# A new order for the first microseconds, and a shorter head weighting, in a linear-attention and Mish kernel

## The chip, the cores and the metric

The kernel runs on one core of a Trainium2 chip. The metric is the device time of one execution in microseconds (us); lower is better. A core has TensorE (PE in the profile; PEld is its weight load), VectorE (DVE), ScalarE (ACT), GpSimd (POOL) and SyncE (SP, which here only issues DMAs). Each engine works through its own list of instructions in order, and waits where an instruction needs a result that another engine or a DMA hasn't delivered.

## The reference

The input `x` has 2048 rows of 512 numbers. The kernel computes `x + A(xn) + B(xn)` in bf16.

```
xn = layernorm(x)                                   # (x - mean) / sqrt(var + 1e-5)
# A: linear attention, 32 heads of 16
q, k, v = split(xn @ wqkv)
pq, pk  = q @ w_phi[h],  k @ w_phi[h]               # a 16x16 matrix per head
phi     = concat(softmax(p), softmax(-p))           # 32 features, for q and for k
kv, z   = sum_s phi_k^T v,  sum_s phi_k
A       = concat_heads(phi_q kv / (phi_q z + 1e-6)) @ wo
# B: a dense layer with Mish, width 1792
B       = mish(xn @ w1 + b1) @ w2
```

## The kernel before, in words

The 2048 rows are 16 tiles of 128 rows, in four groups of four. The order of all work is written out by hand: each engine's list follows the order of the calls in the source, and a PSUM bank comes from a pool (`bank`, L66) in a fixed rotation `turns`, so that TensorE waits when the bank whose turn it is hasn't been read out.

The projection of q and k is folded with the per-head matrices: `fold` (L105) multiplies the transposed weight `wT` by a block-diagonal matrix `Wbd` (made at L477 from `block`, a mask, and `wsrc`, the loaded `w_phi`) and copies four PSUM banks into `wkp`. From then on `project(wkp, t)` (L163) gives the logits of tile t directly, and `logits` (L203) copies them to `p_sb`.

**The head** (L443 to L511) deals with group 0. After the DMAs are issued, GpSimd makes the identity and the mask, and TensorE runs twelve matmuls on the identity that nobody reads (L471). `ln_stats` (L122) takes mean and variance on VectorE for two tiles at a time, and GpSimd turns the variance into 1/sqrt by an addition and a power (L131, L134). `ln_apply` (L137) normalises on VectorE. Then come the fold of the k weights (three casts on ScalarE, one on VectorE), `ln_turn_pe` (L149: four transposes of a tile on TensorE into one bank, then a copy to `xnT`), and the logits of the four tiles. Next VectorE takes the statistics of group 1, starts `extremes(0)` (L211: the maximum and the minimum of each run of 16 logits, then the differences `e`) and in the middle of it normalises group 1, which a DMA transposes (L158). In the meantime TensorE computes the values of four tiles and five units of the hidden layer (`hidden`, L183: four matmuls, then a Mish on ScalarE, L196, which reads the bank). There are 56 such units in all. TensorE can be at most as many units ahead of ScalarE as there are banks.

**First half** (L513 to L557): for each group, ScalarE takes the exponentials of `e` (L244), VectorE divides by the sums (`normalise`, L258), TensorE accumulates k and v (L290), and projections, hidden units and the statistics of later groups fill the rest.

**Second half** (L560 to L652): `attend(h, i)` (L324) multiplies the transposed query features by the accumulated matrix into a four-bank tile `pnd`. ScalarE copies out of it first the 32 features' numerators `nm` (L347, which lands in the buffers of `wkp` or `wv`), then the denominators `ds` (L348). `combine(h)` (L350) works on VectorE, in two parts of one tile or in one part of two: products `u` of the denominators (L370), their sum `w` (L373), its reciprocal (L376), weights `u` again (L379, an instruction per tile), the same weights written twice side by side as `f` in bf16 (L382), `nm` times `f` (L389), and the sum of the two planes (L396). A DMA then transposes the result into `ob` (L399). `second_layer` (L407, L415) and `project_out` (L420, L424) accumulate into one bank per tile, and `residual` (L430, L432) adds it to x on VectorE. All sixteen output tiles leave by DMA (L440).

Of the kernel before, what the change touches and what calls it, by code (L numbers as in the profile page):

```python
# [13 lines left out]
ALU = mybir.AluOpType  # L14
# [4 lines left out]
def kernel(  # L19
# [68 lines left out]
    wo_sb = wqk[:, :, D : 2 * D]  # L88
    ident = consts.tile([P, P], BF16, name="ident")
    mhalf = consts.tile([P, TPG], FP32, name="mhalf")  # L90
    block = consts.tile([P, 8, 16], BF16, name="block")
    KVmask = consts.tile([P, 34], FP32, name="KVmask")
    vext = [vpool.tile([P, TPG, 4, 4, 36], BF16, name=f"vext{i}") for i in range(2)]
# [8 lines left out]
        nc.sync.dma_start_transpose(out=wT[:], in_=A_wqkv[:, base_col : base_col + D])  # L102
        return wT

    def fold(wT, dst, dve):  # L105

        for kt in range(KT):
            pf = bank("pfold")
            for j in range(4):
                nc.tensor.matmul(  # L110
                    pf[:, j * P : (j + 1) * P],
                    lhsT=wT[:, j, kt * P : (kt + 1) * P],
                    rhs=Wbd[:, j, :],
                    start=True,
                    stop=True,
                )
            if kt in dve:
                nc.vector.tensor_copy(dst[:, kt, :], pf[:])
            else:
                nc.scalar.copy(dst[:, kt, :], pf[:])  # L120

    def ln_stats(t0, n):  # L122

        stats = lnp.tile([P, TPG, nc.vector.BN_STATS_DIM], FP32, name="stats")
        mv = lnp.tile([P, TPG, nc.vector.BN_AGGR_DIM], FP32, name="mv")
        rstd = lnp.tile([P, TPG], FP32, name="rstd")
        for i in range(n):
            nc.vector.bn_stats(stats[:, i, :], x_sb[:, t0 + i, :])  # L128
        for i in range(n):
            nc.vector.bn_aggr(mv[:, i, :], stats[:, i, :])  # L130
        nc.gpsimd.tensor_scalar(  # L131
            out=rstd[:, 0:n], in0=mv[:, 0:n, 1], scalar1=1e-5, scalar2=None, op0=ALU.add
        )
        nc.gpsimd.tensor_tensor(out=rstd[:, 0:n], in0=rstd[:, 0:n], in1=mhalf[:, 0:n], op=ALU.pow)  # L134
        return mv, rstd
# [24 lines left out]
            in_=xn[:, i : i + 2, :].rearrange("p t c -> p (t c)"),  # L160
        )

    def project(w, t, pp=None):  # L163

        if pp is None:
            pp = bank("pproj")[:]
        for kt in range(KT):
            nc.tensor.matmul(  # L168
                pp, lhsT=xnT[:, t, kt, :], rhs=w[:, kt, :],
                start=(kt == 0), stop=(kt == KT - 1),  # L170
            )
        return pp
# [151 lines left out]
    def attend(h, i):  # L324

        if i == 0:
            nd_of[h] = (
                (wkp, wv)[h % 2][:].rearrange("p (i l) c -> p i l c", i=2),
                opool.tile([P, 2, 2, 4, 4, 4], FP32, name="ds"),
            )  # L330
        nm, ds = nd_of[h]
        pnd = later[0].tile([P, 4, 512], FP32, name="pnd", tag="nd")
        for pl in range(2):
            for j in range(4):
                for r in range(4):
# [11 lines left out]
        nc.scalar.copy(to, a[:, :, :, :, 0:32])  # L347
        nc.scalar.copy(ds[:, i], a[:, :, :, :, 32:36])  # L348

    def combine(h, parts=(slice(0, 2),)):  # L350

        nm, ds = nd_of.pop(h) if parts[-1].stop == 2 else nd_of[h]
        ds = ds[:].rearrange("p i l j r (x h) -> p i l x (j r) h", x=2)
        if h not in oT_of:
            ob = lnp.tile([P, 4, 512], BF16, name="ob", tag="xn")
            u = opool.tile([P, 2, 2, 32], FP32, name="u")
            w = opool.tile([P, 2, 32], FP32, name="w")
            f = opool.tile([P, 2, 2, 32, 2], BF16, name="f")
            tmp_of[h] = ob[:, 0:2, :], u, w, f
            oT_of[h] = ob[:, 2:4, :].rearrange("p i (j c) -> p (i j) c", c=P)  # L360
        o_t, u, w, f = tmp_of[h]
        for q in parts:
            n = q.stop - q.start
            uh = u[:, q].rearrange("p i l (c h) -> p i l c h", h=2)
            wh = w[:, q, None, :].to_broadcast([P, n, 2, 32]).rearrange(
                "p i l (c h) -> p i l c h", h=2
            )
            for i in range(n):
                k = q.start + i
                nc.vector.tensor_tensor(  # L370
                    out=uh[:, i], in0=ds[:, k, :, 0], in1=ds[:, k, ::-1, 1], op=ALU.mult
                )
            nc.vector.tensor_tensor(  # L373
                out=w[:, q], in0=u[:, q, 0, :], in1=u[:, q, 1, :], op=ALU.add
            )
            nc.vector.reciprocal(w[:, q], w[:, q])  # L376
            for i in range(n):
                k = q.start + i
                nc.vector.tensor_tensor(  # L379
                    out=uh[:, i], in0=ds[:, k, ::-1, 1], in1=wh[:, i], op=ALU.mult  # L380
                )
            nc.vector.tensor_copy(  # L382
                f[:, q].rearrange("p i l c o -> p (i l c) o"),
                u[:, q].rearrange("p i l (c o) -> p (i l c) o", o=1).to_broadcast(
                    [P, n * 64, 2]
                ),
            )
# [8 lines left out]
            nc.vector.tensor_tensor(  # L396
                out=o_t[:, q], in0=nm[:, q, 0, :], in1=nm[:, q, 1, :], op=ALU.add
            )
# [54 lines left out]


    make_identity(nc, ident[:])

    nc.gpsimd.memset(block[:], 1.0)
    for sign in (1, -1):
# [5 lines left out]
    nc.gpsimd.memset(mhalf[:], -0.5)  # L464
    for i in range(2):
        nc.gpsimd.memset(vext[i][:, :, :, :, 32:36], 1.0)
    dve, act = nc.vector.tensor_copy, nc.scalar.copy

    warm = bank("warm")
    for _ in range(12):  # L470
        nc.tensor.matmul(  # L471
            warm[:].rearrange("p (k c) -> p k c", k=4), lhsT=ident[:], rhs=ident[:, None, :].to_broadcast([P, 4, P]),
            start=True, stop=True,
        )

    st0 = ln_stats(0, 2)
    nc.vector.tensor_tensor(  # L477
        out=Wbd[:].rearrange("p j (h e) -> p j h e", h=8),
        in0=block[:, None, :, :].to_broadcast([P, 4, 8, 16]),
        in1=wsrc[:, :, None, :].to_broadcast([P, 4, 8, 16]),  # L480
        op=ALU.mult,
    )
# [25 lines left out]
    nc.sync.dma_start(wo_sb, wo_v[:, :, :])  # L508
    for i in range(TPG):
        value(i, act)  # L510
    hidden(5)  # L511

    for s in range(NG):  # L513
        exponentials(s, (0, 1) if s else (0,))
# [32 lines left out]
        if s == 0:  # L547
# [135 lines left out]
```

## Time and profile before

| what | value |
|---|---|
| median of 3 runs | 181.95 us (181.59 to 182.17) |
| the profiled execution | 181.76 us |
| its span, from the first to the last instruction | 179.8 us |
| outside the span | 1.96 us |
| granted TensorE clock, mean | 0.997 |
| busy share: TensorE, VectorE, ScalarE, GpSimd | 95%, 86%, 69%, 16% |
| busy TensorE outside 0 to 6.5 us and 165 to 180 us | 154.8 of 158.5 us |

A timeline row of the profile gives the start in us, the busy time of the row in us, the engine, the source line, the operation, `out<-in` with the shapes, and the number of instructions that were merged into it; in brackets stands how long the engine was idle just before, and what released it. Lines are those of the kernel before. A row of a view by groups ends in the total busy time in us and the mean ns of one instruction, then idle time and its releaser. A matmul of 512 columns lasts 0.38 us in these rows, but the next one starts 0.216 us after it, since matmuls are pipelined.

### The profile page before, as it was taken

The numbers are of one execution on the slowest core, as the hardware profiler recorded it, in microseconds if no ns is written. First come the engines' busy times: TensorE is split into PE (matmuls) and PEld (weight loads), VectorE is DVE, ScalarE is ACT, GpSimd is POOL, SyncE is SP. The second block draws the span as 40 slices with busy tenths as digits, with TensorE's granted clock in tenths as the row PEclk, the third lists the DMA queues.
The fourth block names the chain that finished last, engine by engine and source line by source line (L and its number), as shares of the span: only waits on it lengthen the run. The fifth ranks groups of instructions, "written<-read, shape, count | busy, mean of one in ns | idle before, by whom it ended". The sixth has DMA issues, their size and how long they took to land.

```text
span 179.8 us, 4310 instructions
## 1 busy us (share of the span) xinstructions
PE 170.8 (95%) x1785; PEld 81.8 (46%) x1807; DVE 154.0 (86%) x313; ACT 123.9 (69%) x162; POOL 29.6 (16%) x42
## 2 busy tenths in 40 slices
PE   6799999999999999999999999899999999998993
PEld 2454443454444545544454444344444444443561
DVE  1989979997999989998999959799899978798853
ACT  2367999999998899969994987379223863543200
POOL 4404069400799300000000000000000000000000
PEclk9999999999999999999999999999999999999998
DMA  5997796300023600000000692809945078386334
GB/s 145 295 400 277 165 343 180 69 5 4 4 53 64 120 0 4 0 4 0 0 4 0 129 108 60 120 5 145 227 115 99 0 136 130 88 86 154 62 91 142
DMA packets 44527, 18.12 MB, mean 101 GB/s; under 512 B 36956, under 2 KB 43996, under 8 KB 44508
## 3 DMA queue, kind: packets, MB, share of 16 engines
q1 hardware_dynamic: 43536, 17.50, 44.4%
q10 hardware_dynamic: 972, 0.35, 0.7%
q8 instruction: 14, 0.23, 0.5%
q14 instruction: 5, 0.04, 0.1%
HBM read 6.84 MB, written 2.10 MB: 50 GB/s over the span
## 4 chain that ended last, share of the span: by engine, by line
DVE 47%; PE 33%; ACT 8%; DMA 8%; issue 2%; DVEq 0%; ACTq 0%; SPq 0%
PE po L415 14%; DVE s L262 7%; DVE m L225 6%; PE po L424 6%; PE ph L189 6%; PE pproj L168 5%; ACT e L244 5%; DVE stats L128 5%; DVE e L234 5%; DVE e L275 4%; DMA ob<-ob 4%; DVE r L270 3%; DMA qT<-e 2%; DVE x_sb L432 2%; DMA x_sb<-in_A_x_dram 2%
## 5 line engine op out<-in xcount | busy, mean ns | idle before, releaser
L415 PE MATMUL po<-w_sb,acts 128*128 128x512 bf16 (+1 forms) x224 | 50.2, 366 | 0.8 <-PE pnd L337 0.2
L189 PE MATMUL ph<-xnT,w_sb 128*128 128x512 bf16 x224 | 49.5, 379 | 0.4 <-ACT acts L196 0.4
L196 ACT ACTIVATE acts<-ph,b1f 128x512 bf16<-128x512 f32 x56 | 34.7, 705 | 2.0 <-PE ph L189 1.9
L244 ACT ACTIVATE e<-e 128x2048 bf16<-128x2048 bf16 x16 | 30.2, 1911 | 6.5 <-DVE e L234 6.4
L189 PEld LDWEIGHTS <-w_sb 128*128 128x128 bf16 x224 | 21.8, 98 | 26.8 <-issue 0.7
L415 PEld LDWEIGHTS <-acts 128*128 128x128 bf16 x238 | 22.2, 98 | 22.5
L168 PEld LDWEIGHTS <-xnT 128*128 128x128 bf16 x192 | 18.2, 98 | 22.0 <-DMA xnT<-xn 0.8
L262 DVE TENSOR_REDUCE s<-e 128x128 f32<-128x2048 bf16 x8 | 18.2, 2278 | 2.5 <-ACT e L244 2.5
L347 ACT CAST wv<-pnd 128x1024 bf16<-128x1024 f32 x8 | 8.1, 1010 | 14.5 <-PE pnd L337 12.3
L140 POOL TENSOR_SCALAR xn<-x_sb,mv,rstd 128x512 bf16<-128x512 bf16 x8 | 16.7, 2102 | 0.2
L424 PE MATMUL po<-wqk,ob 128*128 128x512 bf16 (+1 forms) x67 | 15.1, 367 | 1.3 <-DMA ob<-ob 1.2
L432 DVE TENSOR_TENSOR x_sb<-po,x_sb 128x512 bf16<-128x512 f32 (+1 forms) x17 | 11.0, 658 | 5.7 <-PE po L424 5.7
L168 PE MATMUL pproj<-wv,xnT 128*128 128x512 bf16 x61 | 14.8, 380 | 0.2
L209 ACT CAST p_sb<-pproj 128x512 bf16<-128x512 f32 x21 | 11.3, 587 | 4.9 <-PE pproj L168 4.9
L168 PE MATMUL pproj<-wqk,xnT 128*128 128x512 bf16 x62 | 14.4, 379 | 0.3 <-DVE x_sb L432 0.2
L225 DVE TENSOR_TENSOR m<-m 128x256 bf16<-128x256 bf16 (+2 forms) x44 | 13.4, 305 | 1.5
L128 DVE BATCH_NORM_STATS2 stats<-x_sb 128x6 f32<-128x512 bf16 x16 | 10.0, 680 | 3.8 <-DMA x_sb<-in_A_x_dram 3.8
L168 PE MATMUL pproj<-wkp,xnT 128*128 128x512 bf16 x50 | 11.8, 379 | 0.1
L347 ACT CAST wkp<-pnd 128x1024 bf16<-128x1024 f32 x8 | 8.1, 1014 | 3.5 <-PE pnd L337 3.4
L275 DVE TENSOR_TENSOR e<-e,r 128x2048 bf16<-128x2048 bf16 x8 | 10.3, 1282 | 0.3
L424 PEld LDWEIGHTS <-ob 128*128 128x128 bf16 x68 | 6.4, 98 | 8.3 <-DMA ob<-ob 1.8
L225 DVE TENSOR_TENSOR m<-p_sb 128x1024 bf16<-128x1024 bf16 (+1 forms) x18 | 10.2, 565 | 0.0
(66 smaller groups left out, 170.2 us busy)
## 6 DMA issues: line engine op xcount, KB each, us to landing
w_sb<-in_B_w_dram SPq DMA_DIRECT2D x2, 1792.0 KB, 8.9
out_dram<-x_sb SPq DMA_DIRECT2D x15, 128.0 KB, 1.9
x_sb<-in_A_x_dram SPq DMA_DIRECT2D x1, 1024.0 KB, 11.4
x_sb<-in_A_x_dram SPq DMA_DIRECT2D x1, 512.0 KB, 4.4
wv<-in_A_wqkv_dram SPq DMA_DIRECT2D x1, 512.0 KB, 5.2
wqk<-in_A_wo_dram SPq DMA_DIRECT2D x1, 512.0 KB
x_sb<-in_A_x_dram SPq DMA_DIRECT2D x1, 256.0 KB, 3.0
x_sb<-in_A_x_dram ACTq DMA_DIRECT2D x1, 256.0 KB, 3.3
```

Of the source, the lines that this page charges most:

```text
L128: nc.vector.bn_stats(stats[:, i, :], x_sb[:, t0 + i, :])
L140: engine.tensor_scalar(out=xn[:, at + i, :], in0=x_sb[:, t0 + i, :], scalar1=mv[:, i, 0:1], scalar2=rstd[:, i : i + 1], op0=ALU.subtract, ...
L168: nc.tensor.matmul(pp, lhsT=xnT[:, t, kt, :], rhs=w[:, kt, :], start=(kt == 0), stop=(kt == KT - 1),)
L189: nc.tensor.matmul(ph[:], lhsT=w1_sb[:, kt, f * P : (f + 1) * P], rhs=xnT[:, g * TPG : (g + 1) * TPG, kt, :], start=(kt == 0), stop=(kt == ...
L196: nc.scalar.activation(acts[:, f, g * 512 : (g + 1) * 512], ph[:], ACT.Mish, bias=b1f[:, f : f + 1])
L225: nc.vector.tensor_tensor(out=m, in0=src[:, :, 0:half], in1=src[:, :, half : 2 * half], op=op)
L244: nc.scalar.activation(v, v, ACT.Exp)
L262: nc.vector.reduce_sum(t[:], v.rearrange("p t l (c e) -> p (t l c) e", e=16), axis=AX.X)
L275: nc.vector.tensor_tensor(out=vv, in0=vv, in1=r2[:, :, None, :].to_broadcast([P, 128, 8, 2]), op=ALU.mult)
L347: nc.scalar.copy(to, a[:, :, :, :, 0:32])
L415: nc.tensor.matmul(po[:, c], lhsT=acts[:, f, t * P : (t + 1) * P], rhs=w2_sb[:, f, c], start=(f == 0), stop=False,)
L424: nc.tensor.matmul(po[:, c], lhsT=oT_of[h][:, t % 2 * 4 + j, :], rhs=wo_sb[:, j, c], start=False, stop=(j == 3),)
```

## The change

In the head, `1/sqrt` of the variance is no longer taken on GpSimd by a power but as a square root on ScalarE and a reciprocal on VectorE. Tiles 0 and 1 get their statistics, root and normalisation one by one, tiles 2 and 3 follow together. The transposes of tile 0 stand ahead of the fold, the fold is split into two pairs, the logits of tile 1 are split around the transposes of tile 2. `Wbd` is multiplied on GpSimd instead of VectorE. Three more PSUM banks (`hd`) serve the head, so that eight are in rotation. Eleven instead of twelve idle matmuls run first. The first batch of hidden units is six instead of five, and a later one four instead of five.

In `attend` the denominators are copied ahead of the numerators, and into an order that lies by half, plane and head. In `combine` the products of two tiles are one instruction, and the weights are multiplied straight into the doubled `f`, which removes L379's intermediate and the copy L382.

```diff
+    eps = consts.tile([P, 1], FP32, name="eps")
+    root = consts.tile([P, 1], FP32, name="root")
...
-    def fold(wT, dst, dve):
-        for kt in range(KT):
+    def fold(wT, dst, dve, kts=range(KT)):
+        for kt in kts:
...
-    def project(w, t, pp=None):
+    def project(w, t, pp=None, kts=range(KT)):
...
-                opool.tile([P, 2, 2, 4, 4, 4], FP32, name="ds"),
+                opool.tile([P, 2, 2, 64], FP32, name="ds"),
...
+        nc.scalar.copy(
+            ds[:, i].rearrange("p x (g r h) -> p g r x h", g=8, r=4),
+            pnd[:, :, 0:288].rearrange("p r (g c) -> p g r c", g=8)[:, :, :, 32:36].rearrange(
+                "p g r (x h) -> p g r x h", x=2
+            ),
+        )
         nc.scalar.copy(to, a[:, :, :, :, 0:32])
-        nc.scalar.copy(ds[:, i], a[:, :, :, :, 32:36])
...
-            for i in range(n):
-                k = q.start + i
-                nc.vector.tensor_tensor(
-                    out=uh[:, i], in0=ds[:, k, :, 0], in1=ds[:, k, ::-1, 1], op=ALU.mult
-                )
+            nc.vector.tensor_tensor(
+                out=u[:, q], in0=ds[:, q, 0], in1=ds[:, q, 1, ::-1], op=ALU.mult
+            )
...
             nc.vector.reciprocal(w[:, q], w[:, q])
-            for i in range(n):
-                k = q.start + i
+            for k in range(q.start, q.stop):
                 nc.vector.tensor_tensor(
-                    out=uh[:, i], in0=ds[:, k, ::-1, 1], in1=wh[:, i], op=ALU.mult
+                    out=f[:, k],
+                    in0=ds[:, k, 1, ::-1, :, None].to_broadcast([P, 2, 32, 2]),
+                    in1=w[:, k, None, :, None].to_broadcast([P, 2, 32, 2]),
+                    op=ALU.mult,
                 )
-            nc.vector.tensor_copy(
-                f[:, q].rearrange("p i l c o -> p (i l c) o"),
-                u[:, q].rearrange("p i l (c o) -> p (i l c) o", o=1).to_broadcast([P, n * 64, 2]),
-            )
...
     make_identity(nc, ident[:])
+    nc.gpsimd.memset(eps[:], 1e-5)
+    nc.scalar.activation(root[:], eps[:], ACT.Sqrt)
...
-    for _ in range(12):
...
-    st0 = ln_stats(0, 2)
-    nc.vector.tensor_tensor(
+    nc.gpsimd.tensor_tensor(
         out=Wbd[:].rearrange("p j (h e) -> p j h e", h=8),
...
-    st1 = ln_stats(2, 2)
-    ln_apply(0, 2, *st0, xn, 0)
-    fold(wT, wkp, (3,))
-    ln_turn_pe(0, xn, 0, dve)
-    ln_turn_pe(1, xn, 1, act)
-    pb = bank("pb", BF16)
-    nc.tensor.transpose(pb[:, 0:FT], b1b[:], ident[0:FT, 0:FT])
-    ln_apply(2, 2, *st1, xn, 2)
-    logits(0, 0, act)
-    for i in range(2, 4):
-        ln_turn_pe(i, xn, i, dve)
-    nc.vector.tensor_copy(b1f[:], pb[:, 0:FT])
-    for i in range(1, TPG):
-        logits(0, i, act)
+    head, hd = three_banks("hd", 3)
+    turns[0] = cycle([hd, ps, hd, px, ps, hd, ps, ps])
+    for _ in range(11):
...
+    def spread(t):
+        nc.vector.bn_stats(stats[:, t, :], x_sb[:, t, :])
+    def gather(t, n):
+        for i in range(t, t + n):
+            nc.vector.bn_aggr(mv[:, i, :], stats[:, i, :])
+    def deviate(t, n):
+        nc.scalar.activation(rstd[:, t : t + n], mv[:, t : t + n, 1], ACT.Sqrt, bias=eps[:])
+    def invert(t, n):
+        nc.vector.reciprocal(rstd[:, t : t + n], rstd[:, t : t + n])
+    def apply(t):
+        nc.vector.tensor_scalar(
+            out=xn[:, t, :], in0=x_sb[:, t, :], scalar1=mv[:, t, 0:1], scalar2=rstd[:, t : t + 1],
+            op0=ALU.subtract, op1=ALU.mult,
+        )
+    for t in (0, 1):
+        spread(t)
+        gather(t, 1)
+        deviate(t, 1)
+    for t in (0, 1):
+        invert(t, 1)
+        apply(t)
+    ln_turn_pe(0, xn, 0, act)
+    spread(2)
+    spread(3)
+    gather(2, 2)
+    fold(wT, wkp, (), (0, 1))
+    deviate(2, 2)
+    fold(wT, wkp, (2,), (2, 3))
+    ln_turn_pe(1, xn, 1, dve)
+    invert(2, 2)
+    apply(2)
+    apply(3)
+    logits(0, 0, act)
+    p1 = project(wkp, 1, kts=range(0, 2))
+    ln_turn_pe(2, xn, 2, dve)
+    act(p_of[0][:, 1, :], project(wkp, 1, p1, kts=range(2, 4)))
+    ln_turn_pe(3, xn, 3, dve)
+    pb = bank("pb", BF16)
+    nc.tensor.transpose(pb[:, 0:FT], b1b[:], ident[0:FT, 0:FT])
+    nc.vector.tensor_copy(b1f[:], pb[:, 0:FT])
+    for i in range(2, TPG):
+        logits(0, i, act)
+    head.close()
+    turns[0] = cycle([px, ps, ps, ps, ps])
...
-    hidden(5)
+    hidden(6)
...
-        hidden((5, 14, 8, 10)[s])
+        hidden((4, 14, 8, 10)[s])
```

More of the change, by code (lines that the diff above doesn't have):

```diff
@@ L161, in ln_turn_dma @@
         )
-    def project(w, t, pp=None):
+    def project(w, t, pp=None, kts=range(KT)):
         if pp is None:
             pp = bank("pproj")[:]
-        for kt in range(KT):
+        for kt in kts:
             nc.tensor.matmul(
@@ L346, in attend @@
         to = nm[:, i, :, :].rearrange("p l (j r c) -> p l j r c", j=4, r=4)
+        nc.scalar.copy(
[4 more added lines that the diff above has]
+        )
         nc.scalar.copy(to, a[:, :, :, :, 0:32])
-        nc.scalar.copy(ds[:, i], a[:, :, :, :, 32:36])
     def combine(h, parts=(slice(0, 2),)):
         nm, ds = nd_of.pop(h) if parts[-1].stop == 2 else nd_of[h]
-        ds = ds[:].rearrange("p i l j r (x h) -> p i l x (j r) h", x=2)
+        ds = ds[:].rearrange("p i x (l c) -> p i x l c", l=2)
         if h not in oT_of:
@@ L363, in combine @@
             n = q.stop - q.start
-            uh = u[:, q].rearrange("p i l (c h) -> p i l c h", h=2)
-            wh = w[:, q, None, :].to_broadcast([P, n, 2, 32]).rearrange(
-                "p i l (c h) -> p i l c h", h=2
-            )
-            for i in range(n):
-                k = q.start + i
-                nc.vector.tensor_tensor(
-                    out=uh[:, i], in0=ds[:, k, :, 0], in1=ds[:, k, ::-1, 1], op=ALU.mult
-                )
+            nc.vector.tensor_tensor(
+                out=u[:, q], in0=ds[:, q, 0], in1=ds[:, q, 1, ::-1], op=ALU.mult
+            )
             nc.vector.tensor_tensor(
@@ L376, in combine @@
             nc.vector.reciprocal(w[:, q], w[:, q])
-            for i in range(n):
-                k = q.start + i
+            for k in range(q.start, q.stop):
                 nc.vector.tensor_tensor(
-                    out=uh[:, i], in0=ds[:, k, ::-1, 1], in1=wh[:, i], op=ALU.mult
-                )
-            nc.vector.tensor_copy(
-                f[:, q].rearrange("p i l c o -> p (i l c) o"),
-                u[:, q].rearrange("p i l (c o) -> p (i l c) o", o=1).to_broadcast(
-                    [P, n * 64, 2]
-                ),
-            )
+                    out=f[:, k],
+                    in0=ds[:, k, 1, ::-1, :, None].to_broadcast([P, 2, 32, 2]),
+                    in1=w[:, k, None, :, None].to_broadcast([P, 2, 32, 2]),
+                    op=ALU.mult,
+                )
             v = nm[:, q].rearrange("p i l (c e o) -> p (i l c) e o", e=8, o=2)
@@ L466 @@
         nc.gpsimd.memset(vext[i][:, :, :, :, 32:36], 1.0)
-    dve, act = nc.vector.tensor_copy, nc.scalar.copy
-    warm = bank("warm")
-    for _ in range(12):
[L471 to L474, printed above, removed]
-    st0 = ln_stats(0, 2)
-    nc.vector.tensor_tensor(
+    nc.gpsimd.tensor_tensor(
         out=Wbd[:].rearrange("p j (h e) -> p j h e", h=8),
@@ L482 @@
     )
-    st1 = ln_stats(2, 2)
-    xn = lnp.tile([P, TPG, D], BF16, name="xn", tag="xn")
-    ln_apply(0, 2, *st0, xn, 0)
-    fold(wT, wkp, (3,))
-    ln_turn_pe(0, xn, 0, dve)
-    ln_turn_pe(1, xn, 1, act)
+    dve, act = nc.vector.tensor_copy, nc.scalar.copy
+    head, hd = three_banks("hd", 3)
+    turns[0] = cycle([hd, ps, hd, px, ps, hd, ps, ps])
+    warm = bank("warm")
+    for _ in range(11):
+        nc.tensor.matmul(
+            warm[:].rearrange("p (k c) -> p k c", k=4), lhsT=ident[:], rhs=ident[:, None, :].to_broadcast([P, 4, P]),
+            start=True, stop=True,
+        )
@@ new lines @@
+    xn = lnp.tile([P, TPG, D], BF16, name="xn", tag="xn")
+    stats = lnp.tile([P, TPG, nc.vector.BN_STATS_DIM], FP32, name="stats")
+    mv = lnp.tile([P, TPG, nc.vector.BN_AGGR_DIM], FP32, name="mv")
+    rstd = lnp.tile([P, TPG], FP32, name="rstd")
+    def spread(t):
[5 more added lines that the diff above has]
+        nc.scalar.activation(rstd[:, t : t + n], mv[:, t : t + n, 1], ACT.Sqrt, bias=eps[:])
```

## The prediction

> **What bounds the kernel now.** I read the page's shares first, then who TensorE waited for, then the timeline of the stages that the change touches.
>
> ```profile
> PE 170.8 (95%) x1785; PEld 81.8 (46%) x1807; DVE 154.0 (86%) x313; ACT 123.9 (69%) x162; POOL 29.6 (16%) x42
> ...
> PE po L424 <- DMA ob<-ob: 1.2, 2, 0.6
> PE pfold L110 <- DMA wT<-in_A_wqkv_dram: 0.8, 1, 0.8
> PE ptr L152 <- DVE wkp L118: 0.6, 1, 0.6
> PE ph L189 <- ACT acts L196: 0.4, 1, 0.4
> ...
> PE pproj L168 <- DVE x_sb L432: 0.2, 1, 0.2
> ```
>
> TensorE is the bound. Its list of waits (total, times, longest) is short: apart from the start-up only five entries matter, and none lies between 29 and 102 us. So time is won only where a wait goes or where useful work begins sooner, and everything behind moves as a block if the other engines keep up. The entries fall in the head (L110, L152), in the first hidden units (L189) and in the second half (L424, L432).
>
> ```profile
> 0.79 0.48 ACTq L445 DMA_DIRECT2D wsrc<-in_A_w_phi_dram  x1
> ...
> 2.33 0.56 POOL L466 MEMSET vext<- 128x256 bf16 x2
> ...
> 3.82 1.29 DVE L128 BATCH_NORM_STATS2 stats<-x_sb 128x6 f32<-128x512 bf16 x2 [3.82 <-DMA x_sb<-in_A_x_dram]
> ...
> 5.24 0.41 DVE L477 TENSOR_TENSOR Wbd<-block,wsrc 128x512 bf16<-128x512 bf16 x1
> ...
> 6.57 1.07 PE L110 MATMUL pfold<-Wbd,wT 128*128 128x128 bf16 x16 [0.76 <-DMA wT<-in_A_wqkv_dram]
> ...
> 7.00 1.56 ACT L120 CAST wkp<-pfold 128x512 bf16<-128x512 f32 x3 [3.09 <-PE pfold L110]
> ...
> 8.41 0.38 PE L152 MATMUL ptr<-ident,xn 128*128 128x128 bf16 x4 [0.56 <-DVE wkp L118]
> ...
> 8.84 1.04 PE L168 MATMUL pproj<-wkp,xnT 128*128 128x512 bf16 x4
> ...
> 10.88 2.46 DVE L128 BATCH_NORM_STATS2 stats<-x_sb 128x6 f32<-128x512 bf16 x4
> ...
> 12.75 3.62 PE L168 MATMUL pproj<-wv,xnT 128*128 128x512 bf16 x16
> ```
>
> Two streams leave the head: TensorE begins the values at 12.75, VectorE begins group 1's statistics at 10.88. The fold can't begin before 6.57, where its weights land; the change leaves that DMA where it was.
>
> **The head after the change.** I replay it with the durations above and these (last two numbers ahead of the second bar: busy us, mean ns):
>
> ```profile
> L140 DVE TENSOR_SCALAR xn<-x_sb,mv,rstd 128x512 bf16<-128x512 bf16 x8 | 2.8, 404 | 0.0
> ...
> L155 DVE COPY xnT<-ptr 128x512 bf16<-128x512 bf16 x3 | 1.2, 418 | 0.8 <-PE ptr L152 0.8
> ...
> L130 DVE BATCH_NORM_AGGREGATE mv<-stats 128x2 f32<-128x6 f32 x8 | 1.0, 164 | 0.0
> ...
> L118 DVE CAST wkp<-pfold 128x512 bf16<-128x512 f32 x1 | 0.7, 690 | 0.0
> ```
>
> VectorE: from the statistics rows (1.29 for two, 2.46 for four) one costs 0.59 more, 0.70 alone. Tile 0's mean and variance stand at 4.70, tile 1's at 5.48. Small roots on ScalarE have no row; below, the smallest ScalarE row is 0.29 (a copy of 128x128), and a copy of 128x512 in the row above has a pitch of 0.49. I take 0.28 and keep 0.5 as the other end. So the roots are ready at 5.04 and 5.84. A reciprocal of one element has no row either; the aggregate (0.16) is nearest, and I take it. VectorE then normalises tile 0 by 6.10 and tile 1 by 6.63. Statistics of tiles 2 and 3 last to 8.05, the cast of the third weight bank (0.69) to 8.66, the copy of tile 1's transposes (0.42) to 9.05, tile 2 is normalised at 9.55 and tile 3 at 9.90.
>
> TensorE: the transposes of tile 0 (0.38) now fit between 6.15 and 6.55, inside the wait for the weights. The fold keeps its 6.57 to 7.64, and tile 1's transposes follow at once, since eight banks leave none to wait for. ScalarE copies tile 0 at 6.6, then the first two weight banks at a pitch of 0.49 (done 7.70, 8.18), then the root of tiles 2 and 3, which waits until 8.05, then the last bank (done 8.9). That last cast ends the wait of the first logits: TensorE is through them at 9.15 (before: 8.84 plus 4 x 0.216 = 9.70). Half of tile 1's logits, transposes at 9.60, the other half, transposes at 10.26 and the logits of tiles 2 and 3 follow with hardly a gap, and the values begin at about 12.28 instead of 12.75. The head gives **x = 0.47 us**. Its bounds: 0.95 if the wait of 0.56 and the 0.38 of transposes go wholly; about -0.3 if each root costs 0.5 and each of the hand-overs among three engines 0.1 more.
>
> VectorE's last copies now wait for transposes that come in two steps: done at 11.13, so group 1's statistics begin about 0.25 later than 10.88, although `Wbd` (0.41) has left VectorE (the three reciprocals take back 0.48).
>
> **`Wbd` on GpSimd** has no row of its own. GpSimd is free at 2.33 + 0.56 + 0.1 = 3.0; `wsrc` lands at 0.79 + 3.2 = 3.99.
>
> ```profile
> wsrc<-in_A_w_phi_dram ACTq DMA_DIRECT2D x1, 16.0 KB, 3.2
> ...
> L140 POOL TENSOR_SCALAR xn<-x_sb,mv,rstd 128x512 bf16<-128x512 bf16 x8 | 16.7, 2102 | 0.2
> L317 POOL COPY kvm<-block 32x16 bf16<-32x16 bf16 x4 | 2.0, 507 | 0.0
> L316 POOL CAST KVmask<-block 32x2 f32<-32x2 bf16 x4 | 1.2, 296 | 0.0
> ```
>
> The same engine takes 2.10 us for a tile of 128x512; then `Wbd` stands at 6.1 and the wait for `wT` hides it, with 0.4 to spare. The other end comes from the copies that repeat short runs: 14 elements more cost 0.21 us, 15 ns each, which would be 7.7 us for 512. The new product repeats too, but in runs of 16; I take 2.10, which has the size, and keep 0.4 (VectorE's time) and 7.7 as ends. The Trainium skill speaks against this move: GPSIMD Engine Reference, section 4.1, wants elementwise multiplies on VectorE, with GpSimd about twice as slow for two inputs; its section 3.1 gives some 2.6 cycles an element, by which I estimate 1.1 us plus dispatch. No row here shows such a product; by it the sum would be the same.
>
> **The hidden units.** Six units instead of five put 4 x 0.216 = 0.86 us more of work ahead of group 1's logits and 0.62 more on ScalarE ahead of the exponentials.
>
> ```profile
> 17.00 1.28 ACT L196 ACT_TABLE_LOAD   x1
> ...
> 18.30 3.11 ACT L196 ACTIVATE acts<-ph,b1f 128x512 bf16<-128x512 f32 x5
> ...
> 20.58 0.82 PE L168 MATMUL pproj<-wkp,xnT 128*128 128x512 bf16 x3
> ...
> 22.72 1.91 ACT L244 ACTIVATE e<-e 128x2048 bf16<-128x2048 bf16 x1
> ...
> 28.96 10.52 PE L189 MATMUL ph<-xnT,w_sb 128*128 128x512 bf16 x48 [0.39 <-ACT acts L196]
> ...
> 41.62 0.69 DVE L176 CAST vext<-pproj 128x512 bf16<-128x512 f32 x1 [1.37 <-PE pproj L168]
> ```
>
> At 28.96 TensorE waited for ScalarE, which was late with Mish because the exponentials stood ahead of it. ScalarE's whole row from 17.00 on moves by 0.62 - x = +0.15: exponentials at 22.87, the bank free at 29.11. TensorE reaches group 1's logits at 20.58 - 0.47 + 0.86 = 20.97, just when their transposes land (20.58 + 0.25 = 20.83), and waits at 28.7 until 29.11, with one unit more behind it. Gain of the first half: 0.86 - 0.15 = 0.24 + x = **0.71 us**, with x's bounds between -0.06 and 1.2. What would be late next is VectorE, whose division by the sums hangs on those exponentials and starts 0.15 later; it had idled 1.37 us before 41.62, so 0.71 + 0.15 fit.
>
> The table row is the place of a second rule: the Trainium skill, ScalarE: Activation LUTs, section "Table sets: the hidden batching unit", says that roots and exponentials lie in different sets and that each switch costs a load. If the root added a load to the three sets in use, its 1.28 us would stand in the head; but the changed order has one load ahead of the first root and none behind it until Mish, in the place of the load that stood ahead of the first cast. I price it at nothing.
>
> **The second half.** Denominators first lets VectorE do `u`, `w`, the reciprocal and `f` while ScalarE still copies the numerators.
>
> ```profile
> 103.87 1.01 ACT L347 CAST wkp<-pnd 128x1024 bf16<-128x1024 f32 x1
> 104.76 0.29 ACT L348 COPY ds<-pnd 128x128 f32<-128x128 f32 x1
> 105.08 0.23 DVE L370 TENSOR_TENSOR u<-ds 128x64 f32<-128x64 f32 x1 [1.88 <-ACT ds L348]
> ...
> 109.65 0.43 DVE L396 TENSOR_TENSOR ob<-wkp 128x512 bf16<-128x512 bf16 x1
> ...
> 110.11 4.20 DMA ob<-ob
> ...
> 114.35 1.04 PE L424 MATMUL po<-wqk,ob 128*128 128x512 bf16 x4 [0.61 <-DMA ob<-ob]
> ...
> 136.26 3.61 PE L168 MATMUL pproj<-wqk,xnT 128*128 128x512 bf16 x16 [0.15 <-DVE x_sb L432]
> ...
> 164.82 1.90 PE L424 MATMUL po<-wqk,ob 128*128 128x512 bf16 x8 [0.59 <-DMA ob<-ob]
> ...
> L379 DVE TENSOR_TENSOR u<-ds,w 128x64 f32<-128x64 f32 x16 | 3.3, 223 | 0.5
> ...
> L382 DVE CAST f<-u 128x128 bf16<-128x128 f32 x10 | 2.3, 226 | 0.3
> ```
>
> With `ds` at 103.87, VectorE begins at 104.17 instead of 105.08, 0.9 sooner. Per tile the weights cost one instruction of 128 elements instead of 223 + 226 ns and the gap between them. It has no row: between 0.23 and 0.45, and I take 0.28, so 0.2 saved a part. The second `ob` then leaves at 110.11 - 0.9 - 2 x 0.2 = 108.8 and, at 4.20, lands at 113.0. TensorE's last matmul had ended at 114.35 - 0.61 = 113.74, and the next may start 0.38 - 0.216 = 0.16 before such an end, at 113.6; so the whole wait goes, 0.7 by starts. At 136.26 VectorE had a queue of three parts ahead of the residual: 3 x 0.2 off it ends the wait, 0.15 as shown and up to 0.3 by starts; I take 0.25. At 164.82 the whole of `combine(5)` hangs on TensorE's own residual, so only the saved instructions count: 0.2 of 0.59 goes. Together **1.15 us**, between 0 and 1.7.
>
> **Sum:** 0.71 + 1.15 = 1.9 us. The profiled execution took 181.76, of which 179.8 is span; after, 179.9 with a span of 177.9. It lay 0.19 below the median, so against the median the forecast is 181.95 - 1.9 = **180.0 us**.
>
> **Rivals.** (1) *The head gives nothing*: the root between ScalarE's casts holds the last one back, x is -0.2, and the first half gives 0.05. For it speaks that the first logits hang on casts of two engines in turn; against it, that TensorE's work of 0.38 is hidden for certain. Time 181.95 - 0.05 - 1.15 = 180.7. (2) *The earlier `ob` lands no earlier*, because its 4.20 us, long beside the work of one transpose, is waiting for other transposes in SP's queue; then 0.7 of the second half is lost: 181.95 - 0.71 - 0.45 = 180.8. (3) *`Wbd` comes late*: all sixteen fold matmuls wait for GpSimd. From 2.5 us on it delays the fold; at 4.6 us it has eaten the gain of 1.9, and at 6 us, inside the bounds of 0.4 to 7.7, the fold starts at 10.0, 3.4 late, and the time is 181.95 - 1.9 + 3.4 = 183.4, slower. Against it stands the 2.10 row; for it, the repeated operand. (4) *The change doesn't do what it says*: the doubled write of `f` costs 0.45, so `combine` is no shorter; the 0.9 of the reordered copy still frees the wait at 114, and 0.45 is lost: 181.95 - 0.71 - 0.70 = 180.5.
>
> **How the numbers follow.** Forecast 0.62 (its own range 179.1 to 180.9), rival 1 0.13, rival 2 0.08, rival 4 0.06, rival 3 0.11. No change means within 0.3%, 0.55 us, about what a measurement of this kernel can tell: 181.4 to 182.5. Rivals 1, 2 and 4 lie on the faster side, but two or three of them together reach into it, which takes 0.09 from that side: 0.80 for faster, 0.09 for no change, 0.11 for slower. The range is 179.0 to 181.8: below, the upper ends of two terms; above, rivals 1, 2 and 4 nearly all at once (181.95 - 0.05 = 181.9). Rival 3 stays outside.
>
> **What would show it.** In the changed profile: the fold still at 6.57 released by the DMA of `wT` and not by GpSimd; the transposes of tile 0 ahead of it; the first row of values near 12.3; the wait of `ph` for Mish near 29.1, with eleven units behind it; the wait of L424 near 113 gone and the one of 0.59 near 163 down to 0.4. I am wrong if GpSimd's product exceeds 2.5 us, if the last weight cast ends after 9.3, or if VectorE, at 86%, fails to move with TensorE between 43 and 97 us.

## The result, and the profile after

| | median (range) | executions |
|---|---|---|
| before | 182.12 us (181.59 to 182.42) | 6 |
| after | 181.12 us (180.96 to 181.63) | 6 |

The ratio is 0.9952, with a 95% interval of 0.9933 to 0.9972: faster by 0.9 us (1.0 by the medians), where 1.9 us less than the median of before was forecast. The kernel is faster, as forecast, but half of the gain is missing.

The waits of TensorE in the kernel after (total, times, longest) are those that the forecast wanted: the fold's and the transposes' waits are gone, and so is one of the two for `ob`, but the wait for Mish has grown.

```profile
PE warm L478 <- POOL eps L453: 1.4, 1, 1.4
PE ph L191 <- ACT acts L198: 0.5, 1, 0.5
PE po L421 <- DMA ob<-ob: 0.5, 1, 0.5
PE po L412 <- PE pnd L339: 0.2, 1, 0.2
```

The timeline after, with the rows that answer to those of before; the last is the output's third-last residual, with which the tail begins:

```profile
4.32 1.15 POOL L466 TENSOR_TENSOR Wbd<-block,wsrc 128x512 bf16<-128x512 bf16 x1 [1.39 <-DMA wsrc<-in_A_w_phi_dram]
...
4.96 0.29 ACT L496 ACTIVATE rstd<-mv,eps 128x1 f32<-128x1 f32 x1 [0.84 <-DVE mv L493]
...
6.69 1.32 PE L112 MATMUL pfold<-Wbd,wT 128*128 128x128 bf16 x16
...
12.66 3.62 PE L170 MATMUL pproj<-wv,xnT 128*128 128x512 bf16 x16
...
29.74 9.66 PE L191 MATMUL ph<-xnT,w_sb 128*128 128x512 bf16 x44 [0.51 <-ACT acts L198]
...
104.97 0.29 DVE L379 TENSOR_TENSOR f<-ds,w 128x128 bf16<-128x128 f32 x1
...
112.63 1.90 PE L421 MATMUL po<-wqk,ob 128*128 128x512 bf16 x8
114.45 3.63 PE L170 MATMUL pproj<-wqk,xnT 128*128 128x512 bf16 x15
...
135.18 3.18 PE L170 MATMUL pproj<-wqk,xnT 128*128 128x512 bf16 x14
...
163.62 1.90 PE L421 MATMUL po<-wqk,ob 128*128 128x512 bf16 x8 [0.47 <-DMA ob<-ob]
...
174.63 1.35 DVE L429 TENSOR_TENSOR x_sb<-po,x_sb 128x512 bf16<-128x512 f32 x3 [0.17 <-PE po L421]
```

To see where the time went I cut both spans at three places: the first accumulation (`pkv`, 39.41 before, 39.33 after), the first `pnd` (102.44, 102.30) and the third-last residual (175.84, 174.63). The head gained 0.08, the middle 0.06, the second half 1.07. But from the residual to the end of the span (179.76 before, 179.51 after, with one more digit) it took 3.92 us before and 4.88 after: **0.96 us were given back in this tail**, behind the second half that the change shortens, and where it edits nothing.

The list of DMAs in the window 176 to 178 us shows it (KB each, us to landing). First before, then after:

```profile
q1 hardware_dynamic: 331, 0.29, 41.8%
q10 hardware_dynamic: 98, 0.05, 8.2%
...
out_dram<-x_sb SPq DMA_DIRECT2D x1, 64.0 KB, 1.5
```

```profile
q1 hardware_dynamic: 285, 0.20, 30.1%
q10 hardware_dynamic: 144, 0.07, 11.6%
q14 instruction: 1, 0.01, 2.2%
...
out_dram<-x_sb SPq DMA_DIRECT2D x1, 64.0 KB, 2.6
```

The last store of 64 KB lands 2.6 us after its issue instead of 1.5, and a transfer of another queue has come into its window: q14, an instruction fetch of 8192 bytes. In the records of single packets it starts at 177.16 and takes 0.71 us; the last eight packets of the store (512 bytes, 27 ns each) follow one another from 177.87 on, while all others had started by 177.19. The eight start at the moment when the fetch ends (177.16 + 0.71 = 177.87), and so they do in all four other profiles with a fetch there: at 177.58 in e3, 177.29 in e4, 178.49 in e5 and 177.71 in e10, the runs below. Eight is a sixteenth of the store's 128 packets, and the core has 16 DMA engines; so I read the eight as the share of one engine, which had to move the fetch first. Before, the last fetch of q14 came at 180.1, behind all work.

### The profile page after: what moved, and what is told of

Its sections match the earlier page's. It is cut to its first block, busy times and chain, and to the rows that moved or that the text cites. A ratio compares the mean times of both kernels' runs of the same rounds, so it can differ in the third digit from the quotient of the medians.

```text
span 179.5 us, 4305 instructions
## 1 busy us (share of the span) xinstructions
PE 171.5 (96%) x1784; PEld 82.4 (46%) x1806; DVE 152.1 (85%) x299; ACT 124.8 (70%) x166; POOL 29.0 (16%) x40
## 4 chain that ended last, share of the span: by engine, by line
PE 51%; DVE 31%; ACT 10%; DMA 4%; issue 2%; POOL 0%; DVEq 0%; POOLq 0%; ACTq 0%; SPq 0%
PE po L412 21%; PE pproj L170 9%; PE ph L191 8%; DVE s L264 7%; PE po L421 7%; ACT e L246 5%; DVE m L227 5%; DVE e L277 4%; DVE e L236 4%; DVE r L272 3%; PE warm L478 3%; PE pnd L339 2%; DMA qT<-e 2%; DMA ob<-ob 2%; ACT acts L198 1%
## 5 line engine op out<-in xcount | busy, mean ns | idle before, releaser
L349 ACT COPY ds<-pnd 128x128 f32<-128x128 f32 x16 | 4.4, 276 | 18.1 <-PE pnd L339 15.8
L211 ACT CAST p_sb<-pproj 128x512 bf16<-128x512 f32 x20 | 10.8, 587 | 3.8 <-PE pproj L170 2.3
L170 PE MATMUL pproj<-wkp,xnT 128*128 128x512 bf16 x50 | 12.3, 379 | 0.2
L236 DVE TENSOR_TENSOR e<-p_sb,m 128x2048 bf16<-128x2048 bf16 (+1 forms) x9 | 8.9, 990 | 0.3
L236 DVE TENSOR_TENSOR e<-m,p_sb 128x2048 bf16<-128x2048 bf16 (+1 forms) x9 | 8.9, 988 | 0.3
```

The lines of the kernel that those rows point to most:

```text
L170: nc.tensor.matmul(pp, lhsT=xnT[:, t, kt, :], rhs=w[:, kt, :], start=(kt == 0), stop=(kt == KT - 1),)
L236: nc.vector.tensor_tensor(out=e[:, :, pl, :].rearrange("p t (c e o) -> p t c e o", e=8, o=2), in0=p5 if pl == 0 else mb, in1=mb if pl == 0 ...
```

## The experiments

The theory after this profile: the change adds instructions to ScalarE's list, so the list's next fetch comes earlier and falls into the last stores. Its rivals: the second half gives less than it seems; the sixth hidden unit and the head cost what was lost; the late store is chance. Every kernel was timed together with the kernel before (median 182.0 to 182.2 in each set); ratios are to that. Positions in time come from one profiled execution of each.

**Half by half.** e1 has the new `attend` and `combine` with the old head; e2 has the new head with the old `attend` and `combine`.

> The kernel before with only the new attend and combine (denominators first, weights multiplied straight into f). Theory A, the second half carries nearly all of the gain: the two traces gain 1.07 us between the first pnd (L337) and the last residual, so 0.9 to 1.2 us faster than before, with the wait of L424 for ob near 114 gone. Rival B, the recorded forecast's split: also 1.15. If the time falls by less than 0.5, the 1.07 is lost again behind the last residual, in the stores.

> The changed kernel with the old attend and combine, so the head and the move of one hidden unit alone. Theory A, the head gives only the shift x of the first values, since the sixth Mish waits for TensorE's sixth unit: 0.0 to 0.3 us faster than before, and the wait of the hidden units for Mish ends 0.87 - x later than before. Rival B, the recorded forecast: 0.71 us faster. Rival C, the late clock of the one profile was chance: the first values near 12.3 and 0.4 to 0.5 faster.

Measured: e1 180.58 us (ratio 0.9907, 0.9893 to 0.9921), e2 181.70 (0.9969, 0.9955 to 0.9983). Alone the halves gain 1.6 and 0.5, together 1.0. Half of the change is faster than the whole. From the first `pnd` to the third-last residual e1 took 174.69 - 102.45 = 72.24, 1.16 less than before: the forecast's 1.15. The tail took 3.8 in e1 and 3.7 in e2, and neither has a fetch in it (e1's starts at 179.44, and in e2 none of q14 starts after 165.8). Both gains are larger than theory A had them. For e1 the two profiled executions differ by 1.2 us; the other 0.4 is that the profiled execution of before (181.76) lies that much below the median of before in this set (182.19). For e2 (0.5, not 0.0 to 0.3) the cause of the rest is open; its values begin at 12.60.

**Five units, and the same again.**

```diff
-    hidden(6)
+    hidden(5)
...
-        hidden((4, 14, 8, 10)[s])
+        hidden((5, 14, 8, 10)[s])
```

> The changed kernel with five hidden units in the first batch and five later, as before. Theory A (the sixth unit only moves work: its Mish waits for TensorE, and the exponentials wait for it): same time as the changed kernel within 0.15 us, with exponentials about 0.75 us earlier than its 23.5 and a wait for group 1's transposes near 20.6 in their place. Rival B, the recorded forecast: 0.24 us slower than the changed kernel, since the unit fills a wait.

> The changed kernel once more, for a second profile. In the first one the idle matmuls never left the pitch of 0.43 us, and the last store took 2.6 us. Theory A: both vary from execution to execution; here the matmuls reach 0.21 us at some time between 4.8 and 8 us, the last store takes about 1.6, and the span is near 179.0. Rival C: eleven instead of twelve idle matmuls keep the clock low in every execution, and the same pitch of 0.43 us is seen up to the transposes.

Measured: e3 181.44 (0.9955, 0.9939 to 0.9971), e4 181.15 (0.9938, 0.9926 to 0.9951). The first accumulation stands at 39.15 in e3 and 39.13 in e4, so in these profiles the sixth unit buys next to nothing; by the medians e3 is 0.29 slower, not within 0.15, but the intervals overlap. Both have the late last store (2.7 and 2.4, where theory A had 1.6 for e4), so the lost time repeats. The idle matmuls of e4 keep the pitch of 0.43 us, as in the first profile, while the same eleven in e3 come down to 0.22: that varies by execution.

**Moving ScalarE's list.** e5 drops one ScalarE instruction, the first root, whose output nobody reads. e6 adds eight copies of one column where ScalarE idles 2.4 us, and e8 adds four to e1 at the same place. The first line is e5's, the others are e6's, with 4 for 8 in e8:

```diff
-    nc.scalar.activation(root[:], eps[:], ACT.Sqrt)
...
+    for _ in range(8):
+        nc.scalar.copy(root[:], eps[:])
     exponentials(4)
```

> The changed kernel without the first square root on ScalarE, whose output nobody reads; one ScalarE instruction fewer ahead of everything. Theory (an instruction fetch of ScalarE's list, set off by the count of its instructions, delays the last store's packets): the sixth fetch comes one instruction later, about 0.5 us, at 177.3 to 177.8 us or after the end of the work; the last store then lands in 1.5 to 2.6 us; 0.2 to 0.9 us faster than the changed kernel's 181.1. Rival (the fetch belongs to another engine's list or falls where it likes): the fetch stays at 176.8 to 177.2 and the time within 0.2 us.

> The changed kernel with eight copies of one column on ScalarE ahead of the last group's exponentials, where ScalarE idles 2.4 us. Theory: the fetch comes eight ScalarE instructions earlier, at 165 to 172 us, clear of the last store; that store lands in about 1.5 us instead of 2.6 and the time is 0.6 to 0.9 us below the changed kernel's 181.1: 180.2 to 180.5. Rival (the fetch is not ScalarE's, or chance): fetch near 177 and the time equal to the changed kernel's, or up to 0.5 us longer for the eight copies.

> The second half's change alone (180.58 us before) with four copies of one column on ScalarE ahead of the last group's exponentials, which idle time covers. Theory: four instructions more bring the fetch, seen at 179.4 behind the end of the work, forward into the last stores at 176 to 177.5; the last store lands in 2.1 to 2.6 us instead of 1.5; 0.4 to 0.9 us slower than 180.58. Rival (the late store of the changed kernel comes from the new head in another way): the fetch stays behind the end and the time within 0.2 us of 180.58.

The table has the profiled execution of each, and in its last column the median time.

| kernel | fetch starts (us) | behind the third-last residual | last store lands after | tail | time |
|---|---|---|---|---|---|
| e1 | 179.44 | 4.75 | 1.5 | 3.8 | 180.58 |
| e8, four more than e1 | 177.87 | 2.83 | 1.5 | 3.8 | 180.35 |
| e4, the changed kernel | 176.88 | 2.53 | 2.4 | 4.6 | 181.15 |
| e5, one fewer than e4 | 177.71 | 2.44 | 2.6 | 4.8 | 182.13 |
| e6, eight more than e4 | 157.8 | -16.6 | 1.5 | 3.8 | 180.34 |

e6 settles the tail: eight copies of ScalarE more make the changed kernel 0.8 us *faster* (ratio to before 0.9904, 0.9887 to 0.9921). The tails of e4, then of e6, in the list of DMAs from 176 to 178 us:

```profile
q14 instruction: 1, 0.01, 1.3%
...
out_dram<-x_sb SPq DMA_DIRECT2D x1, 64.0 KB, 2.4
```

```profile
q1 hardware_dynamic: 287, 0.20, 29.8%
q10 hardware_dynamic: 144, 0.07, 11.6%
...
out_dram<-x_sb SPq DMA_DIRECT2D x1, 64.0 KB, 1.5
```

No q14 is left in e6's window. e8 (ratio 0.9902, 0.9883 to 0.9921) came out half as expected: the four copies moved the fetch forward by 1.9 us against the residual, so it is ScalarE's, but it started 0.28 us behind the last packet (177.59), and the expected 0.4 to 0.9 us of loss did not come. That e8 is even 0.23 below e1 has another place: its spans (178.5 to 178.8) are no shorter than e1's (178.4 to 178.5), but the time outside the span is 1.7 us in all six executions of e8, and 1.9 to 2.2 in those of all other kernels. Why, no run shows.

e5 (ratio 0.9999, 0.9984 to 1.0013) missed, for two reasons: with one instruction fewer the fetch starts no later against the residual (2.44 us behind it, 2.53 in e4), so the store stays late, and the head lost 0.9. ScalarE's rows of e5 show what that unread root does:

```profile
4.92 1.28 ACT L495 ACT_TABLE_LOAD   x1 [4.92 <-DVE mv L492]
6.21 0.48 ACT L495 ACTIVATE rstd<-mv,eps 128x1 f32<-128x1 f32 x2
```

With the unread root, the load of 1.28 us ran at 2.62, while ScalarE had nothing to do; without it, the load waits for the first variance, and the values begin at 13.40 instead of 12.47. The Trainium skill, ScalarE: Activation LUTs, "Table sets: the hidden batching unit", has each switch between sets cost a load. The row of 1.28 us is such a load, and here it began only when the variance for its root was there. That is no rule: before, the load ahead of the first cast ran at 2.63, though the cast's operand came at 7.00.

**The order of the copies.** e7 is e6 with the numerators copied first, as before; the shorter `combine` stays.

```diff
+        nc.scalar.copy(to, a[:, :, :, :, 0:32])
         nc.scalar.copy(
             ds[:, i].rearrange(...
...
-        nc.scalar.copy(to, a[:, :, :, :, 0:32])
```

> As the run with eight copies, but ScalarE copies the numerators first and the denominators second, as the kernel before did; the shorter combine stays. The prediction gave 0.7 us of the second half's 1.15 to the earlier denominators (the wait at 114) and 0.45 to the shorter combine: then this kernel is 0.6 to 0.7 us slower than the one with eight copies, with a wait of L424 for ob of about 0.4 back near 114. Rival (the shorter combine alone frees the waits): within 0.2 us of the run with eight copies.

Measured: 180.22 (0.9899, 0.9881 to 0.9916), not slower than e6. VectorE starts `u` at 104.87 instead of 103.96, and yet TensorE doesn't wait. The reason is in the landing of the second `ob`: issued only 0.60 us earlier than before (109.51 for 110.11), it lands after 2.4 us, where the kernel before shows 4.20. Denominators first, to which the prediction gave 0.7 us, buy nothing measurable here.

**Why 4.20?** In the kernel before, another q14 fetch starts at 111.96 in the packets of that transpose; in e2, which has the old `combine` too, one at 111.9 goes with a landing after 4.55 and a wait of 0.95 for `ob`; in e1 and in the changed kernel it comes at 118.1 and 118.0. If it is VectorE's, VectorE's list must move it. e9 is the kernel *before* with twelve writes of one column under VectorE's idle 1.88 us.

```diff
+    for _ in range(12):
+        nc.vector.memset(spare[:], 0.0)
     combine(0, first)
```

> The kernel before with twelve writes of one column on VectorE ahead of combine(0, first), where VectorE idles 1.88 us. Theory (the second ob's 4.20 us, where 2.4 is the usual landing, come from an instruction fetch of VectorE at 111.96, in the last packets of that transpose): the fetch comes earlier, at 105 to 110 us, that ob lands in 2.4 us, the wait of L424 at 114.35 (0.61) goes, and the kernel before gets 0.4 to 0.7 us faster: 181.4 to 181.7 against 182.1. Rival (the prediction's: the transpose only starts too late): landing 4.2 us and the wait stay, time within 0.2 us of the kernel before, or up to 0.3 longer.

Measured: 181.45 (0.9973, 0.9959 to 0.9987): twelve useless instructions make the kernel before 0.6 us faster. The q14 fetch moved to 108.44, so it is VectorE's. Before, then e9, each with its fetches in the window 107 to 113 us and its transposes (median us to landing of the two; 3.3 is that of 2.4 and 4.2):

```profile
q8 instruction: 1, 0.02, 1.0%
q14 instruction: 1, 0.01, 0.4%
...
ob<-ob SPq DMA_TRANSPOSE x2, 3.3
```

```profile
q14 instruction: 1, 0.01, 0.5%
...
ob<-ob SPq DMA_TRANSPOSE x2, 2.4
```

Before has a line that e9 lacks, and it isn't the one that I had aimed at: a fetch of 16384 bytes on another queue, q8. It starts at 112.47 before, ahead of the landing at 114.30, and at 113.24 in e9, behind the landing at 112.72. So the edit moved two fetches. There are 14 of q8 in every profile; TensorE, with 1785 matmuls and 1807 weight loads, has by far the longest list, so they are probably TensorE's, but no run moves TensorE's list to show it.

And TensorE's rows of e9, which answer to those at 112.70, 114.35 and 115.22 before: eight matmuls without a gap.

```profile
112.91 1.90 PE L425 MATMUL po<-wqk,ob 128*128 128x512 bf16 x8
114.75 3.61 PE L169 MATMUL pproj<-wqk,xnT 128*128 128x512 bf16 x16
...
135.70 2.53 PE L169 MATMUL pproj<-wqk,xnT 128*128 128x512 bf16 x11 [0.15 <-DVE x_sb L433]
```

**The same in the changed kernel**, from the other side: bring VectorE's fetch into that transpose (e10 on the changed kernel, e12 on e7), and leave ScalarE's list alone as a control for the tail (e10). The edit is that of e9, with 14 and 10 writes.

> The changed kernel with fourteen writes of one column on VectorE ahead of combine(0, first), most of them under its idle 0.97 us. Theory for the middle (a fetch of VectorE's list slows the second ob): the fetch, seen at 117.9, comes to 109.5 to 111 us and the second ob lands 3 to 4.5 us after its issue instead of 2.4; by its earlier start that costs no time, at most 0.2 us. Theory for the end (the fetch at 177 is ScalarE's): it stays within 0.4 us of the last residuals, the last store lands in 2.4 to 2.7 us, and the time stays at 181.1 to 181.4. Rival for the end (any added instructions clear it, by chance or by another engine's count): 180.3 to 180.5 as with eight copies on ScalarE.

> The run with eight copies and numerators first (180.22 us; its second ob is issued at 109.5, its packets run from 110.5 to 111.5 and it lands in 2.4 us), with ten writes of one column on VectorE ahead of combine(0, first), under VectorE's idle 1.88 us. Counted from the run with fourteen writes (fetch at 109.74), ten bring VectorE's fetch to 110.7 to 111.6 us, into or just behind that transpose's packets. Theory (such a fetch holds the transpose back): the second ob lands 3 to 4.5 us after its issue, a wait of 0.1 to 0.4 us at the second tile of L421 comes back, and the time is 180.2 to 180.7. Rival (the 4.2 us of the kernel before had another cause): landing 2.4 us, no wait there, 180.1 to 180.4. Where the fetch misses the packets by more than 0.3 us, the run tells nothing.

Measured: e10 181.30 (0.9955, 0.9938 to 0.9972), e12 180.22 (0.9901, 0.9886 to 0.9917). For the tail the control holds: fourteen instructions on VectorE leave the fetch in the last store (177.18, landing 2.4), and the time is that of the changed kernel. For the middle both missed: the fetch came at 109.74 and 107.91, ahead of the packets, which start about 1 us after the issue at 109.6 and 109.5; landing stayed at 2.4 to 2.5. So e9 shows that the 4.20 and its wait go with an edit of VectorE's list, and no run shows that VectorE's fetch makes them. The traces speak for the other fetch:

| transpose of `ob` | issued | q14 fetch | q8 fetch | lands after |
|---|---|---|---|---|
| second, before | 110.11 | 111.96 | 112.47 | 4.20 |
| second, e2 | 109.96 | 111.89 | 112.23 | 4.55 |
| second, e9 | 110.30 | none | 113.24, behind the landing | 2.42 |
| first, e12 | 107.24 | 107.91 | none | 2.48 |
| sixth, after | 132.16 | none | 133.41 | 4.50 |

In the 14 profiles 176 transposes of `ob` have a landing. 19 of them take over 3.3 us (3.33 to 5.04), and in every one a q8 fetch starts at least 0.8 us behind the issue and 1.8 ahead of the landing; in 14 of the 19 no fetch of q14 touches the time between. The other 157 take at most 3.25, the 16 with a q14 fetch alone at most 3.10. So a q8 fetch goes with late landings without any help of VectorE's; not every one does, since nine more that start 2.5 to 2.6 us behind an issue leave the landing at 3.04 to 3.25. In the kernel before, 18 packets of the next transposes, which start at 113.09 to 113.35, take 0.85 to 1.11 us where their like take at most 0.13; they end together at 114.2, and `ob`, whose own last packet had started at 112.37, lands at 114.30. What stays open: a q14 fetch inside the packets of an `ob` stands in before and e2 alone, together with one of q8, so its share can't be told; and the runs don't show why q8's fetch starts 10.0 us behind the first `pnd` in before and 10.7 in e9. In e7, e10 and e12 it starts only 0.04 to 0.09 us behind the landing, so that numerators first escape it there only narrowly.

**Five units with a clean tail.** e11 is e6 with five units at both places, the edit of e3.

> The changed kernel with the eight copies on ScalarE and five hidden units at both places, as in the kernel before. The sixth unit was priced at 0.24 us in the prediction; if it buys that, 180.6. Theory now (the sixth Mish waits for TensorE, so that nothing is gained): within 0.15 us of 180.34.

Measured: 180.50 (0.9908, 0.9889 to 0.9927) beside 180.34, in ranges that overlap (180.14 to 180.84, 180.31 to 180.45). So the sixth unit isn't told apart from nothing, though both pairs lean the same way (0.29 for e3 and e4, 0.16 here). It trades one wait of TensorE for another: with five units 0.35 (e3) and 0.67 (e11) for group 1's transposes, with six 0.51 for Mish.

The best version is the changed kernel with eight idle copies on ScalarE (e6, e7, e12: 180.2 to 180.3), 0.8 to 0.9 us below the changed kernel and 1.7 to 1.8 below the one before. e8, with the old head, is level with e6 in time (180.35); only its span is 0.4 longer.

## Where the prediction failed, and what held

- **The sum left out the tail.** It ended at 164.82 and let everything behind "move as a block". The block's end moved into ScalarE's instruction fetch, and the last store landed after 2.6 us instead of 1.5: 0.96 lost in the profile, and 0.8 by e6. This is the step that failed: a term put at nothing without a reason. Without it, e6's 180.34 lies 0.3 above the forecast. None of the three signs of being wrong came true, and none of them was about the tail.
- **Second half, 1.15**: the size was right (1.07 in the profile after, 1.16 in e1), but the reason of its greatest term was wrong. The 0.7 at 114 were to come from an `ob` that leaves 1.3 us earlier and lands after the same 4.20. In fact the landing time fell to 2.4, and e9 wins the wait though its `ob` leaves 0.2 later. That the sum came out is luck in this term. Rival 2 doubted the 4.20, but looked for its cause in SP's queue; I had not looked at the list of DMAs for that window, which holds the fetches of q8 and q14. The other 0.45, by the shorter `combine`, hold: from the first `pnd` to the third-last residual e9 takes 72.71, e1 72.24 and e7, with numerators first like e9, 72.18. The wait at 136.26 is gone (e9 still has its 0.15), and the one of 0.59 is 0.47 after and 0.39 in e1. `f` at 0.29 was taken as 0.28.
- **The head, x = 0.47**: measured about 0.3. The values begin at 12.75 to 12.98 with the old head (before, e1, e8, e9; mean 12.88) and at 12.42 to 12.82 with the new one (after, e2 to e4, e6, e7 and e10 to e12; mean 12.55; e5 lacks the first root). In time it is less sure: e6 lies 0.24 below e1, and level with e8. The fold stands within 0.3 of its 6.57, transposes of tile 0 are ahead of it, and roots (0.29 for 0.28) and reciprocals (0.13 for 0.16) cost what was taken; the last weight cast ended at 9.15 instead of 8.9, and in the profiles of after and e10, whose values begin last, the fold's row lasted 1.3 instead of 1.07: its first matmuls have twice the usual pitch (0.11 instead of 0.056). Where the rest went, between the logits of tile 1 and the values, the runs don't separate.
- **The sixth unit, 0.24 beside x**: not there. From the first values to the first accumulation it takes 26.66 us before and 26.67 after. The working moved "ScalarE's whole row" by 0.62 - x, as if ScalarE set the pace of the sixth Mish. ScalarE's rows after show that it waits for TensorE's sixth unit:

```profile
21.50 0.69 ACT L198 ACTIVATE acts<-ph,b1f 128x512 bf16<-128x512 f32 x1 [0.18 <-PE ph L191]
22.20 1.28 ACT L246 ACT_TABLE_LOAD   x1
23.50 1.91 ACT L246 ACTIVATE e<-e 128x2048 bf16<-128x2048 bf16 x1
```

The exponentials begin at 23.50, not 22.87 (before: 22.72), and TensorE waits until 29.74, not 29.11. What six units gain ahead of the logits is given back at that wait. With five, the new head loses a little at the transposes instead (26.73 in e3, 27.01 in e11).

- **`Wbd` on GpSimd** took 1.15 us, not 2.10, and ended at 5.47, hidden. The estimate of 1.1 from the Trainium skill, GPSIMD Engine Reference, section 3.1, was nearer than the row that I took; the rule against the move in its section 4.1 costs nothing here, since the fold waits for other things. Rival 3 falls.
- **Rivals 1 and 4** find no support: the values come 0.3 earlier, and the doubled write of `f` cost 0.29, not 0.45.

## What to carry to other kernels

When a small change moves the time by something that no engine's rows explain, cut the span at a few fixed instructions, and look in the slow stretch at all queues that carry no data of yours: e9 was aimed at one fetch, and a second one moved with it. An edit moves an engine's instruction fetches through its mere count of instructions; test that with a few idle instructions on that engine, in a place where it waits anyway, before crediting or blaming the edit. And where a DMA takes longer than its like (4.20 beside 2.4, 2.6 beside 1.5), ask why before building on an earlier start.

## What the runs showed of the hardware

- A fetch of 8192 bytes (q14) takes 0.3 to 0.9 us in most cases (up to 2.1), and packets of a store wait behind it: the last of the eight starts 0.85 us later than the last of the others. A fetch of 16384 bytes (q8) takes 0.9 to 1.6 us, and the 19 late transposes of `ob` (3.3 to 5.0 us instead of 2.4 to 3.25) all had one start between issue and landing. The Trainium skill, Runtime: NRT & Kernel Launch, "Instruction fetch mechanics", has the lists refilled in blocks by a queue of the sequencer and calls the cost of a crossing "mostly hidden". The views here name no fetch as what an engine waited for, so they can't test this for the engine itself; for a store that meets the fetch it was 0.8 us of the kernel's time.
- One copy of a single column cost ScalarE 0.2 us and one write VectorE 0.12, and eight or twelve of them, in idle time, cost the kernel nothing that shows.
